# Retention and two feed-forward layers on one core: output factors kept whole in DRAM, keys loaded once, 64-row states

## The chip, the cores and the metric

The kernel runs on one core of one Trainium2 chip. The metric is the time of one execution on the device in microseconds. Before the change three executions took 1200.15, 1204.12 and 1204.95 us; the median is 1204.12 us.

## What is computed

```python
B, H, S, D = 4, 8, 768, 64            # attention part
gamma = 1.0 - 2.0 ** (-5.0 - np.arange(H))
for t in range(S):                    # retention: a decayed state per head
    state = gamma * state + outer(k[:, :, t], v[:, :, t])
    y[:, :, t] = D ** -0.5 * q[:, :, t] @ state
x = y as (B * S, H * D)               # 3072 tokens x 512
for w_in, w_out, act in ((512x2048, 2048x512, leaky_relu 0.01),
                         (512x2048, 2048x512, h * sigmoid(1.702 h))):
    x = act(x @ w_in) @ w_out
```

All results are float32. The weights of the two layers arrive as 8-byte floats and are turned into float32 on the chip.

## The kernel before, in words

**Retention.** Each sequence is cut into 6 chunks of 128 tokens, so there are 24 steps. A step loads 1 MB: queries and keys with the head dimension on the partitions (two heads stacked to 128 partitions, 4 pairs), and the keys a second time and the values with tokens on the partitions (`a_load`, L254). TensorE forms the scores of each head (L268, 64 rows each), adds `kv` from decayed keys and values (L299), the output from masked scores and values (L305), and adds queries times state (L309). The state `st` of a pair of heads is a 128x128 tile with two 64x64 blocks on its diagonal and zeros beside them; DVE writes the two blocks with two instructions (L314). Loads run four steps ahead.

**The two layers.** Every product of a layer is a two-by-two block product done in seven block products. Each float32 factor is split into a high part that the engine takes exactly (ACT copies it to the type fp32r) and a low part (DVE subtracts the high part), and three matmuls replace one. `first` (L385) is the product with `w_in` plus the activation: 4 blocks of 768 tokens, 8 pairs of column strips each, so 32 pairs; a pair is seven products of six 384-column matmuls (L410). In a pair the order on TensorE is products 1, 5, 3 (of the pair before), 6, 4 (of the pair before), 2, 7. Around them ACT copies `b<-a` (L473), DVE copies `p<-c` (L479) and adds `c<-b,p`, `g<-b,p` (L437), ACT and in layer 1 also DVE apply the activation (L416, L419, L420), and ACT's queue stores the hidden strip `g` to DRAM (`gd`, L434). `second` (L552) is the product with `w_out`: 3 blocks, seven products of eight steps of six 512-column matmuls (L601), from strips that SP loads back 13 steps ahead; DVE sums strips (L576), ACT and DVE split them (L545, L550).

**Weight preparation** (`Prep`, L96) makes the seven factors of a strip half: two loads of 256 KB, ACT and DVE turn 8-byte words to float32 (L122 to L131), POOL rounds and forms sums (L136, L141), then ACT copies the high part and DVE takes the low part (L150, L153). The result goes either straight into the resident `w` tile, or to DRAM (`store`, L156: two stores of 448 KB). All 16 halves of layer 0's `w_in` and half of layer 1's go straight to `w`; the others are stored as high and low part and loaded later, 1792 KB per strip (`loader`, L685, load at L692).

**What sets the order.** Instructions are written out by hand. `Later` is a clock of ticks: a tick is one product in `first` and one step in `second`; `later.at(n, step)` puts a step's instructions n ticks further on. `Prep.start` uses such offsets (`FAST`), and a new preparation starts every `JIT` or `STORED` ticks. `after(q)` is called when TensorE has finished product 4 of strip q in the last block; SP then loads the next product's strip q into the same `w` tile. Each engine executes its own list in order, and SP's list holds all loads and the preparation's stores.

Of the kernel before, what the change touches and what calls it, by code (L numbers as in the profile page):

```python
# [20 lines left out]
P = 128  # L21
# [33 lines left out]
class Later:  # L55


    def __init__(self):
        self.now = 0
        self.due = {}  # L60

# [3 lines left out]
    def tick(self):  # L65
        for step in self.due.pop(self.now, []):
            step()
        self.now += 1

    def drain(self):  # L70
        while self.due:
            self.tick()


@with_exitstack
def retention_two_ffn(ctx: ExitStack, tc: tile.TileContext, qkv, consts, small, w1i, w1o, w2i, w2o, scratch, out):
# [5 lines left out]
    wd = {(kind, lay): dram.tile([P, n, 2, 2, 7, P], F32, name=f"wd{kind}{lay}")  # L82
          for kind, lay, n in (("o", 0, NQ), ("i", 1, NQ // 2), ("o", 1, NQ))}
# [8 lines left out]
    later = Later()  # L92
# [3 lines left out]
    class Prep:  # L96
# [63 lines left out]

        def start(self, pool, at, dest=None):
# [4 lines left out]
            later.at(at[2], self.sums)  # L166
            later.at(at[3], lambda: self.high_part(dest))
# [6 lines left out]
    FAST = (6, 7, 8, 12, 13, 15)  # L174
# [58 lines left out]
    F_BUFS = 2  # L233
    with ExitStack() as actx:
        prep_p = prep_pool(actx)
        a_in = actx.enter_context(tc.tile_pool(name="a_in", bufs=4))
# [11 lines left out]
        st = [a_c.tile([P, NP, P], F32, name=f"st{i}") for i in range(2)]  # L248
# [5 lines left out]
        def a_load(s):  # L254
            ins[s] = a_in.tile([P, 4, 512], F32, tag="in", name="in")
            n = 2 if s < 3 else 4
            for i in range(0, 4, n):
                nc.sync.dma_start(out=ins[s][:, i : i + n], in_=qkv[s, :, i : i + n])

        def a_scores(s):  # L260
            t = ins[s]
            qT = t[:, 0].rearrange("p (n i) -> p n i", n=NP)
            kT = t[:, 1].rearrange("p (n i) -> p n i", n=NP)
            ps = [ps_a.tile([P, NP, P], F32, tag=f"s{e}", name=f"s{e}") for e in range(2)]
            for n in range(NP):
                for e in range(2):
                    r = slice(D * e, D * e + D)
                    nc.tensor.matmul(out=ps[e][:, n], lhsT=kT[r, n], rhs=qT[r, n], start=True, stop=True,  # L268
# [6 lines left out]
        def a_decay(s):  # L275
# [5 lines left out]
            if c < NC - 1:  # L281
                ks_t[s] = a_t.tile([P, H, D], F32, tag="ks", name="ks")
                nc.gpsimd.tensor_tensor(
                    out=ks_t[s], in0=ins[s][:, 2].rearrange("p (h d) -> p h d", h=H),
                    in1=kdec[:, c, :].unsqueeze(2).to_broadcast([P, H, D]), op=ALU.mult)

        def a_out(s):
# [3 lines left out]
            v = t[:, 3].rearrange("p (n f) -> p n f", n=NP)  # L291
            if c < NC - 1:
                if c == 0:
                    kv_t[b] = ps_a.tile([P, NP, D], F32, tag="kv", name="kv", bufs=2)
# [7 lines left out]
            for n in range(NP):  # L302
                for e in range(2):
                    r = slice(D * e, D * e + D)
                    nc.tensor.matmul(out=o[r, n], lhsT=v[:, n, r], rhs=sm[:, e, n], start=(n == 0),  # L305
                                     stop=(c == 0), skip_group_check=True)
            if c > 0:
                for n in range(NP):
                    nc.tensor.matmul(out=o[:, n], lhsT=st[c % 2][:, n], rhs=qs[:, n], start=False, stop=True,  # L309
                                     skip_group_check=True)  # L310
            if c < NC - 1:
                for e in range(2):
                    r = slice(D * e, D * e + D)
                    nc.vector.tensor_tensor(  # L314
                        out=st[(c + 1) % 2][r, :, r], in0=kv[r],
                        in1=gdec[r, c + 1, :].unsqueeze(2).to_broadcast([D, NP, D]), op=ALU.mult)
# [13 lines left out]
        ins[0] = a_in.tile([P, 4, 512], F32, tag="in", name="in")  # L330
        nc.sync.dma_start(out=ins[0][:, :2], in_=qkv[0, :, :2])
        nc.sync.dma_start(out=cst[:, :H], in_=consts[:, :H])
        nc.sync.dma_start(out=ins[0][:, 2:], in_=qkv[0, :, 2:])
# [3 lines left out]
        a_load(2)  # L337
        a_load(3)
# [10 lines left out]
        for i in range(2):  # L349
            nc.gpsimd.memset(st[i], 0.0)  # L350
# [3 lines left out]
        for s in range(len(steps)):  # L354
# [13 lines left out]
            if s + 4 < len(steps):  # L368
                a_load(s + 4)
# [15 lines left out]
    def first(lay, wt, blocks, g_p, prep, line, after, prepared):  # L385
# [3 lines left out]
        with ExitStack() as c:  # L389
# [24 lines left out]
            def act(src, dst):  # L414
# [393 lines left out]
```

## Time and profile before

| | |
|---|---|
| profiled execution | 1204.84 us |
| its span, first to last instruction | 1203.1 us |
| mean granted clock of TensorE | 0.96 of 2.4 GHz |
| busy PE / DVE / ACT / POOL | 1083.9 / 859.9 / 579.5 / 350.5 us |
| moved by DMA | 263.09 MB, 219 GB/s over the span |
| first product of layer 0 / second | 119.0 to 399.2 / 399.2 to 652.7 us |
| first product of layer 1 / second | 655.5 to 953.4 / 953.4 to 1203.1 us |

The retention fills the time up to 119.0 us. The mean busy shares cover stages with different limits, so they are read stage by stage. A matmul is pipelined: its listed duration overlaps the next one's, and its true rate is the distance between starts.

### The profile page before, as it was taken

The numbers are of one execution on the slowest core, as the hardware profiler recorded it, in microseconds if no ns is written. First come the engines' busy times: TensorE is split into PE (matmuls) and PEld (weight loads), VectorE is DVE, ScalarE is ACT, GpSimd is POOL, SyncE is SP. The second block draws the span as 40 slices with busy tenths as digits, with TensorE's granted clock in tenths as the row PEclk, the third lists the DMA queues.
The fourth block names the chain that finished last, engine by engine and source line by source line (L and its number), as shares of the span: only waits on it lengthen the run. The fifth ranks groups of instructions, "written<-read, shape, count | busy, mean of one in ns | idle before, by whom it ended". The sixth has DMA issues, their size and how long they took to land. (4 is left out here: it accounts for less than half of the span.)

```text
span 1203.1 us, 17472 instructions
## 1 busy us (share of the span) xinstructions
PE 1083.9 (90%) x6081; PEld 964.0 (80%) x6082; DVE 859.9 (71%) x1290; ACT 579.5 (48%) x967; POOL 350.5 (29%) x386
## 2 busy tenths in 40 slices
PE   8877989889889699999997787989989799999997
PEld 6766978879789577887885787989989688888886
DVE  5898577586763278687785599888884388687684
ACT  1333556666653244544543464565552255545543
POOL 2566475575742000000002275363540000000000
PEclk9988999999999889999999799999999899999999
DMA  8985757979889942625246653878779953624422
GB/s 312 335 310 193 243 166 233 332 252 342 306 275 370 362 162 89 227 70 179 102 140 245 210 184 131 302 241 273 255 255 349 328 171 99 214 71 137 143 71 70
DMA packets 136185, 263.09 MB, mean 219 GB/s; under 512 B 12064, under 2 KB 88352, under 8 KB 130848
## 3 DMA queue, kind: packets, MB, share of 16 engines
q1 hardware_dynamic: 99232, 211.62, 51.2%
q10 hardware_dynamic: 36864, 50.35, 11.6%
q8 instruction: 48, 0.79, 0.3%
q14 instruction: 41, 0.34, 0.1%
HBM read 157.59 MB, written 104.33 MB: 218 GB/s over the span
## 5 line engine op out<-in xcount | busy, mean ns | idle before, releaser
L545 ACT CAST op<-g 128x512 fp32r<-128x512 f32 x336 | 201.9, 622 | 189.4 <-PE f L601 50.4
L410 PE MATMUL b<-xf,w 128*128 128x384 f32 x1152 | 239.3, 353 | 54.2 <-DVE c L437 25.9
L550 DVE TENSOR_TENSOR op<-g,op 128x512 fp32r<-128x512 f32 x336 | 224.0, 689 | 61.3 <-ACT op L545 59.0
L410 PEld LDWEIGHTS b<-xf,w 128*128 128x128 f32 x1152 | 210.6, 195 | 67.6 <-DVE c L437 33.4
L410 PE MATMUL a<-xf,w 128*128 128x384 f32 x768 | 166.0, 352 | 14.8 <-DVE xf L224 10.5
L136 POOL TENSOR_TENSOR f<-f,rnd 128x512 int32<-128x512 int32 x64 | 93.0, 1453 | 241.4 <-DVE f L131 80.0
L410 PEld LDWEIGHTS a<-xf,w 128*128 128x128 f32 x768 | 144.1, 197 | 18.3 <-DVE xf L224 11.4
L576 DVE TENSOR_TENSOR g<-g 128x512 f32<-128x512 f32 x192 | 146.0, 760 | 17.3 <-DMA g<-gd 17.3
L141 POOL TENSOR_TENSOR f<-f 128x128 f32<-128x128 f32 x256 | 150.9, 610 | 10.0
L632 POOL TENSOR_TENSOR u<-u 128x1024 f32<-128x1024 f32 x6 | 16.0, 2671 | 467.3 <-DVE u L632 392.5
L601 PE MATMUL d<-op,w 128*128 128x512 f32 x576 | 140.1, 402 | 12.7 <-DVE op L550 11.6
L410 PE MATMUL c<-xf,w 128*128 128x384 f32 x768 | 150.1, 344 | 0.7 <-DVE xf L224 0.7
L601 PEld LDWEIGHTS d<-op,w 128*128 128x128 f32 x576 | 111.2, 194 | 38.6 <-DVE op L550 14.0
L601 PE MATMUL e<-op,w 128*128 128x512 f32 x576 | 136.3, 393 | 5.6 <-DVE op L550 5.6
L410 PEld LDWEIGHTS c<-xf,w 128*128 128x128 f32 x768 | 139.4, 192 | 2.1 <-DVE xf L224 2.1
L601 PE MATMUL f<-op,w 128*128 128x512 f32 x576 | 132.5, 389 | 0.0
L601 PEld LDWEIGHTS e<-op,w 128*128 128x128 f32 x576 | 108.2, 189 | 29.7 <-DVE op L550 7.3
L601 PEld LDWEIGHTS f<-op,w 128*128 128x128 f32 x576 | 108.1, 188 | 22.5
L153 DVE TENSOR_TENSOR f<-f,hi 128x896 fp32r<-128x896 f32 x40 | 53.8, 1345 | 29.2 <-ACT hi L150 29.0
L437 DVE TENSOR_TENSOR g<-b,p 128x384 f32<-128x384 f32 x64 | 35.3, 552 | 52.9 <-DMA gd<-g 29.0
L601 PE MATMUL h<-op,w 128*128 128x512 f32 x288 | 67.0, 390 | 0.0
L601 PEld LDWEIGHTS h<-op,w 128*128 128x128 f32 x288 | 53.8, 188 | 11.0
(72 smaller groups left out, 1177.1 us busy)
## 6 DMA issues: line engine op xcount, KB each, us to landing
gd<-g ACTq DMA_DIRECT2D x256, 192.0 KB, 3.9
g<-gd SPq DMA_DIRECT2D x192, 256.0 KB, 4.4
w<-wdo SPq DMA_DIRECT2D x16, 1792.0 KB, 9.5
in<-qkv SPq DMA_DIRECT2D x21, 1024.0 KB, 6.5
wdo<-hi SPq DMA_DIRECT2D x32, 448.0 KB, 3.3
wdo<-f SPq DMA_DIRECT2D x32, 448.0 KB, 3.3
xr<-xd SPq DMA_DIRECT2D x7, 1536.0 KB, 8.4
raw<-w1i SPq DMA_DIRECT2D x32, 256.0 KB, 5.7
```

What stands on the lines that cost most here:

```text
L136: nc.gpsimd.tensor_tensor(out=self.f.bitcast(I32), in0=self.f.bitcast(I32), in1=r, op=ALU.add)
L141: nc.gpsimd.tensor_tensor(out=f[:, o], in0=f[:, a], in1=f[:, b], op=ALU.subtract)
L153: nc.vector.tensor_tensor(out=self.lo, in0=self.t.bitcast(F32)[:, 1:], in1=self.hi.bitcast(F32), op=ALU.subtract)
L410: nc.tensor.matmul(out=t, lhsT=w[:, k, a], rhs=x[:, b, k], start=(start and m == 0), stop=(m == 5), skip_group_check=True)
L437: nc.vector.tensor_tensor(out=o, in0=x, in1=y, op=ALU.add)
L545: nc.scalar.copy(out=t[:, 0], in_=block_of(raw, *item))
L550: nc.vector.tensor_tensor(out=t[:, 1], in0=block_of(raw, *item), in1=t[:, 0].bitcast(F32), op=ALU.subtract)
L576: nc.vector.tensor_tensor(out=a(*s[0]), in0=a(*s[1]), in1=a(*s[2]), op=s[3])
L601: nc.tensor.matmul(out=t[:, j], lhsT=w[:, j, a], rhs=x[:, b], start=(new and q == 0 and m == 0), stop=(q == NQ - 1 and m == 2), skip_group ...
L632: put = lambda o, x, y, op=ALU.add, e=nc.vector: e.tensor_tensor(out=o, in0=x, in1=y, op=op)
```

## The change

- **Output factors whole.** For `w_out` of both layers the preparation stops after POOL's sums and stores the seven factors once as float32 (448 KB per half). `load_second` loads 896 KB per strip into the low half of `w`, and `split` makes high and low part there: ACT copies each half 5 and 6 ticks after the load's issue, DVE subtracts a tick later. These ticks run on a second clock, `loads`, which goes on from `first` into `second`. The second half of layer 1's `w_in` is still stored as two parts.
- **Keys once.** From step 2 on a step loads 768 KB; TensorE turns the keys with an identity (`a_turn`) and ACT copies them to SBUF. Steps 0 and 1 still load both forms. Loads run six steps ahead.
- **States stacked.** `st` is 128x64 per pair of heads; one DVE instruction writes it, and the product with the queries becomes 8 matmuls on 64 rows and 64 columns instead of 4 on 128x128.
- **Smaller edits.** In layer 1 the strip `g` is taken when DVE writes the gated value, not when the sigmoid is issued; layer 0 issues its store right behind the activation. Buffers and intervals change as in the diff.

```diff
@@ class Later
+        for other in self.along:
+            other.tick()
     def drain(self):
+        along, self.along = self.along, ()
...
@@ class Prep
-                self.hi = self.pool.tile([P, 7, P], F32R, tag="hi", name="hi", bufs=2)
+                self.hi = self.pool.tile([P, 8, P], U32, tag="f", name="hi", bufs=F_BUFS).bitcast(F32R)[:, 1:]
...
+        def store_whole(self):
+            nc.sync.dma_start(out=wd["o", self.lay][:, self.q, self.hh], in_=self.t.bitcast(F32)[:, 1:])
...
             later.at(at[2], self.sums)
+            if self.kind == "o":
+                later.at(at[4], self.store_whole)
+                return
...
-    FAST = (6, 7, 8, 12, 13, 15)
+    FAST = (6, 7, 8, 12, 14, 16)
@@ retention
+    LEAD = 6
-        a_in = actx.enter_context(tc.tile_pool(name="a_in", bufs=4))
+        a_in = actx.enter_context(tc.tile_pool(name="a_in", bufs=LEAD))
-        st = [a_c.tile([P, NP, P], F32, name=f"st{i}") for i in range(2)]
+        st = [a_c.tile([P, NP, D], F32, name=f"st{i}") for i in range(2)]
+        def a_turn(s):
+            t = ps_a.tile([P, NP, P], F32, tag="kt", name="kt", bufs=1)
+            for n in range(NP):
+                nc.tensor.matmul(out=t[:, n], lhsT=ins[s][:, 1, n * P : n * P + P], rhs=ident, is_transpose=True,
+                                 start=(n == 0), stop=True, skip_group_check=True)
+            kT[s] = a_t.tile([P, NP, P], F32, tag="kT", name="kT")
+            nc.scalar.copy(out=kT[s], in_=t)
...
+            if s + 2 < len(steps):
+                a_turn(s + 2)
             if c > 0:
                 for n in range(NP):
-                    nc.tensor.matmul(out=o[:, n], lhsT=st[c % 2][:, n], rhs=qs[:, n], start=False, stop=True,
-                                     skip_group_check=True)
+                    for e in range(2):
+                        r = slice(D * e, D * e + D)
+                        nc.tensor.matmul(out=o[r, n], lhsT=st[c % 2][r, n], rhs=qs[r, n], start=False, stop=True,
+                                         skip_group_check=True)
...
@@ first, layer 1's gate
+                    def product():
+                        dst = tile() if t is None else t
+                        nc.vector.tensor_tensor(out=dst, in0=src, in1=s, op=ALU.mult)
+                        later.at(2, lambda: store(dst))
+                    later.at(1, product)
@@ loads of w_out
+    def load_second(lay):
+        tiles = []
+        def after(q):
+            t = w_tile(q)
+            nc.sync.dma_start(out=t[:, :, 1].bitcast(F32), in_=wd["o", lay][:, q])
+            tiles.append(t)
+            def split(h):
+                hi, lo = t[:, h, 0], t[:, h, 1]
+                nc.scalar.copy(out=hi, in_=lo.bitcast(F32))
+                loads.at(1, lambda: nc.vector.tensor_tensor(out=lo, in0=lo.bitcast(F32), in1=hi.bitcast(F32),
+                                                            op=ALU.subtract))
+            for h in range(2):
+                loads.at(5 + h, lambda h=h: split(h))
...
-    JIT, STORED = 4.25, (5.4, 7.5)
+    JIT, STORED = 4, (4.6, 6.5, 7.5)
...
-    F_BUFS = 3
-    g_p = right.enter_context(tc.tile_pool(name="g", bufs=5, side="right", reuse_waits="tile"))
+    F_BUFS = 4
+    g_p = right.enter_context(tc.tile_pool(name="g", bufs=7, side="right", reuse_waits="tile"))
...
-    F_BUFS = 2
+    F_BUFS = 3
```

The last of these lines and a `g` pool that stays at 5 are layer 1's.

On TensorE, in a step of the retention, the list before read as follows (`st_104` is one of the two state tiles, `s_250` and `s_251` the scores of the even and odd heads):

```order
L299 MATMUL kv<-in,ks 64x64 x8
L305 MATMUL o<-sm,in 64x128 x8
L309 MATMUL o<-qs,st_104 128x128 x4
L268 MATMUL s_250<-in 128x128
L268 MATMUL s_251<-in 128x128
```

In the changed kernel the same place reads (`kt` is the PSUM tile of the turned keys):

```order
L335 MATMUL kv<-in,ks 64x64 x8
L341 MATMUL o<-sm,in 64x128 x8
L292 MATMUL kt<-a_ident,in 128x128 x4
L349 MATMUL o<-qs,st_104 64x128 x8
L304 MATMUL s_282<-in,kT 128x128
L304 MATMUL s_283<-in,kT 128x128
```

Four transposes stand between the output and the product with the state, and that product has twice as many matmuls.

On ACT, one pair in the last block of layer 0's first product read before (stores of `g` are the DMA rows):

```order
L473 COPY b<-a 128x384
L416 ACTIVATE g<-g 128x384
L434 DMA gd_62<-g 128x384
L416 ACTIVATE g<-c 128x384
L434 DMA gd_62<-g 128x384
L416 ACTIVATE g<-b 128x384
L434 DMA gd_62<-g 128x384
L416 ACTIVATE g<-a 128x384
L434 DMA gd_62<-g 128x384
```

and reads now:

```order
L514 COPY b<-a 128x384
L454 ACTIVATE g<-g 128x384
L451 DMA gd_62<-g 128x384
L454 ACTIVATE g<-c 128x384
L451 DMA gd_62<-g 128x384
L748 CAST w<-w 128x896 x2
L454 ACTIVATE g<-b 128x384
L451 DMA gd_62<-g 128x384
L454 ACTIVATE g<-a 128x384
L451 DMA gd_62<-g 128x384
```

Two copies of the split stand behind the activation of `c`; the first of them waits for the load of the strip.

On DVE, where layer 0's second product opens, the list before alternated between sums of strips and low parts:

```order
L550 TENSOR_TENSOR op<-g,op 128x512
L576 TENSOR_TENSOR g<-g 128x512
L550 TENSOR_TENSOR op<-g,op 128x512
L576 TENSOR_TENSOR g<-g 128x512
L550 TENSOR_TENSOR op<-g,op 128x512
```

and now it holds the subtractions of the last two strips of `w` as well:

```order
L617 TENSOR_TENSOR g<-g 128x512
L749 TENSOR_TENSOR w<-w 128x896
L591 TENSOR_TENSOR op<-g,op 128x512
L617 TENSOR_TENSOR g<-g 128x512
L591 TENSOR_TENSOR op<-g,op 128x512
L617 TENSOR_TENSOR g<-g 128x512
L591 TENSOR_TENSOR op<-g,op 128x512
L617 TENSOR_TENSOR g<-g 128x512
L749 TENSOR_TENSOR w<-w 128x896
L591 TENSOR_TENSOR op<-g,op 128x512
L617 TENSOR_TENSOR g<-g 128x512
L749 TENSOR_TENSOR w<-w 128x896
```

The first of the three `w` rows is strip 6's, the other two are strip 7's. Strip 7's second half now stands behind five sums of loaded strips, and the step of the product that uses it is the eighth.

## Rows read from the trace of the kernel before

**Rows 1.** Windows by stage: length; busy PE, PEld, DVE, ACT, POOL; PEclk; DMA share; GB/s

```profile
0.00:119.00 119.00, 94.66 (x1271) 79.78 (x1273) 97.23 (x149) 36.62 (x55) 63.76 (x70) 0.93 0.81 291
119.00:332.00 213.00, 190.03 (x1021) 181.85 (x1020) 149.96 (x202) 128.88 (x223) 129.95 (x149) 0.98 0.78 265
332.00:399.20 67.20, 62.17 (x330) 60.96 (x330) 30.19 (x47) 31.19 (x58) 18.49 (x24) 0.95 0.93 335
399.20:427.00 27.80, 17.53 (x51) 12.93 (x50) 8.16 (x14) 6.32 (x13) 0.00 (x0) 0.72 0.88 347
652.70:877.00 224.30, 193.11 (x1017) 186.30 (x1017) 181.40 (x277) 122.77 (x211) 108.02 (x123) 0.94 0.68 235
877.00:953.40 76.40, 64.81 (x331) 62.75 (x331) 40.36 (x72) 27.18 (x54) 9.89 (x13) 0.91 0.88 316
953.40:966.50 13.10, 11.77 (x49) 9.12 (x50) 8.25 (x15) 5.58 (x10) 0.00 (x0) 1.00 0.97 333
```

**Rows 2.** Chain that ended last: start us, us, engine, tile, line, matmul instructions

```profile
886.03 2.12 PE c L410 x12
...
977.36 10.88 PE f L601 x48
...
1095.88 1.09 PE y L617 x8
```

**Rows 3.** Timeline of PE in the retention: start us, us, line, operation, tiles, count

```profile
24.25 1.16 PE L309 MATMUL o<-qs,st 128*128 128x128 f32 x8
25.34 1.16 PE L268 MATMUL s<-in 64*128 64x128 f32 x16
26.43 0.69 PE L299 MATMUL kv<-in,ks 128*64 128x64 f32 x16
26.95 1.04 PE L305 MATMUL o<-sm,in 128*64 128x128 f32 x16
27.92 1.16 PE L309 MATMUL o<-qs,st 128*128 128x128 f32 x8
```

**Rows 4.** Windows, ten microseconds of the retention, columns as in rows 1

```profile
60.00:70.00 10.00, 6.78 (x112) 5.81 (x110) 9.86 (x13) 3.96 (x6) 8.29 (x8) 1.00 0.99 356
```

**Rows 5.** Groups by line and shape: busy us, mean ns, idle before, releasers

```profile
L153 DVE TENSOR_TENSOR f<-f,hi 128x896 fp32r<-128x896 f32 x40 | 53.8, 1345 | 29.2 <-ACT hi L150 29.0
...
L150 ACT CAST hi<-f 128x896 fp32r<-128x896 f32 x40 | 37.7, 943 | 40.2 <-POOL f L141 37.8 <-issue 1.0 <-ACT g L416 0.5
...
L314 DVE TENSOR_TENSOR st<-kv,smalls 64x256 f32<-64x256 f32 x40 | 16.7, 417 | 0.4
...
L617 PE MATMUL y<-ident,u 128*128 128x128 f32 x96 | 12.7, 275 | 1.8 <-ACT u L665 1.1 <-POOL u L632 0.7
```

**Rows 6.** Waits of PE in layer 0's first product: us in total, times, longest us

```profile
PE b L410 <- ACT b L473: 9.0, 8, 3.9
PE b L410 <- DVE c L437: 8.8, 7, 2.6
```

**Rows 7.** DMA issues in 340 to 430 us: KB each, median us to landing

```profile
w<-wdo SPq DMA_DIRECT2D x8, 1792.0 KB, 9.4
...
gd<-g ACTq DMA_DIRECT2D x31, 192.0 KB, 7.4
```

**Rows 8.** DMA issues over the whole span, columns as in rows 7

```profile
gd<-g ACTq DMA_DIRECT2D x256, 192.0 KB, 3.9
...
wdo<-hi SPq DMA_DIRECT2D x32, 448.0 KB, 3.3
```

**Rows 9.** Timeline of DVE where layer 0's second product opens, idle before in brackets

```profile
419.14 0.69 DVE L576 TENSOR_TENSOR g<-g 128x512 f32<-128x512 f32 x1 [12.10 <-DMA g<-gd]
```

**Rows 10.** Waits of DVE in layer 1's last block, columns as in rows 6

```profile
DVE g L420 <- DMA gd<-g: 16.2, 7, 3.3
DVE g L437 <- DMA gd<-g: 11.8, 3, 7.5
```

**Rows 11.** Timeline of DVE while POOL is idle

```profile
901.50 1.08 DVE L153 TENSOR_TENSOR f<-f,hi 128x896 fp32r<-128x896 f32 x1
```

More of the change, by code (lines that the diff above doesn't have):

```diff
@@ L90, in w_tile @@
         return w_p[n % NQ // (NQ // 2)].tile([P, 2, 2, 7, P], F32R, tag="w", name="w")
-    later = Later()
+    loads = Later()
+    later = Later((loads,))
     class Prep:
@@ L336, in retention_two_ffn @@
         nc.sync.dma_start(out=cst[:, H:], in_=consts[:, H:])
-        a_load(2)
-        a_load(3)
+        for s in range(2, LEAD):
+            a_load(s)
         idle = a_c.tile([P, 512], BF16, name="idle")
@@ L348, in retention_two_ffn @@
         keep_warm(8)
-        for i in range(2):
-            nc.gpsimd.memset(st[i], 0.0)
         a_scores(0)
@@ L412, in product, with hidden, relu, gate @@
                         m += 1
-            def act(src, dst):
-                if lay == 0:
+            def hidden(n, r, f, src=None, made=None):
+                blk, q = pairs[n]
+                cols = slice((2 * blk + r) * T1, (2 * blk + r + 1) * T1)
+                tile = lambda: g_p.tile([P, T1], F32, tag="g", name="g")
+                store = lambda t: nc.scalar.dma_start(out=gd[lay][f * NQ + q][:, cols], in_=t)
+                def relu(src, dst):
                     nc.scalar.activation(out=dst, in_=src, func=AF.Lrelu)
-                else:
+                    store(dst)
+                def gate(src, t):
                     s = u_p.tile([P, T1], F32, tag="sg", name="sg", bufs=3)
                     nc.scalar.activation(out=s, in_=src, func=AF.Sigmoid, scale=1.702)
-                    later.at(1, lambda: nc.vector.tensor_tensor(out=dst, in0=src, in1=s, op=ALU.mult))
-            def hidden(n, r, f, src):
-                blk, q = pairs[n]
-                t = g_p.tile([P, T1], F32, tag="g", name="g")
-                ticks = 0 if lay == 0 else 3
-                if callable(src):
-                    src(t)
-                    later.at(1, lambda: act(t, t))
-                    ticks += 1
-                else:
-                    act(src, t)
-                cols = slice((2 * blk + r) * T1, (2 * blk + r + 1) * T1)
-                later.at(ticks, lambda: nc.scalar.dma_start(out=gd[lay][f * NQ + q][:, cols], in_=t))
+                    def product():
[3 more added lines that the diff above has]
+                    later.at(1, product)
+                if made is not None:
+                    t = tile()
+                    made(t)
+                    later.at(1, lambda: relu(t, t) if lay == 0 else gate(t, t))
+                elif lay == 0:
+                    relu(src, tile())
+                else:
+                    gate(src, None)
             def add(o, x, y):
@@ L504, in first @@
                     product(cur["b"], n, 7, False)
-                    hidden(n, 1, 1, lambda t: add(t, cur["b"], cur["p"]))
+                    hidden(n, 1, 1, made=lambda t: add(t, cur["b"], cur["p"]))
                     form(7)
@@ L711, in prepared @@
         early.append(Early(left, lay))
-    tiles, after = loader("o", 0, NQ)
+    tiles, after = load_second(0)
     first(0, w1, blocks, g_p, prep_p, line, after, lambda: prepared(0))
     right.close()
-    tiles1, after = loader("i", 1, NQ // 2)
+    tiles1, after = load_first(NQ // 2)
     right = ExitStack()
@@ L736, in retention_two_ffn @@
         later.tick()
-    line = [(p, tiles1[p.q], JIT) for p in preps("i", 1)[NQ:]] + [(p, None, STORED[1]) for p in preps("o", 1)]
-    tiles, after = loader("o", 1, NQ)
+    line = [(p, tiles1[p.q], JIT) for p in preps("i", 1)[NQ:]] + [(p, None, STORED[2]) for p in preps("o", 1)]
+    tiles, after = load_second(1)
     first(1, tiles1, blocks, g_p, prep_p, line, after, lambda: prepared(1))
```

65 lines of the change are left out of this document (37 added, 28 removed).

## The prediction

> **What bounds the kernel now.** I read the windows by stage first, then the chain, then the waits of the stages that lose time. TensorE is the engine to count against. In dense stretches 12 of the 384-column matmuls take 2.12 us and 48 of the 512-column ones 10.88 us [rows 2], so a product of `first` costs 1.06 us, a pair of seven 7.42 us, a layer's 32 pairs 237.4 us, and a layer's 1008 wide matmuls 228.5 us. Set against this, the stages lose:
> - Layer 0's `first`: 213.0 us for 24 pairs (178.1), 34.9 lost, and 67.2 us for its last block (59.4), 7.8 lost [rows 1].
> - The opening of layer 0's `second`: 27.8 us for 10.88 us of matmuls, 16.9 lost at a mean granted clock of 0.72 [rows 1].
> - Layer 1's `first`, with the change of layers ahead of it: 224.3 us for 24 pairs, 46.2 lost, and 76.4 us for the last block, 17.0 lost. Its `second` opens in 13.1 us, 2.2 lost [rows 1].
>
> What is late differs by stage. Inside `first` TensorE waits for ACT's copy `b<-a` (9.0 us) and for DVE's sum `c` (8.8 us) [rows 6]: both engines work in order and stand in the weight preparation; ACT's high-part copies alone wait 37.8 us for POOL's sums [rows 5]. In both last blocks DMA is the limit: share 0.93 and 0.88 [rows 1], a load of `w` takes 9.4 us, and a 192 KB store of `g` 7.4 us there [rows 7] against 3.9 over the span [rows 8]. The stores hold the `g` buffers, and DVE in layer 1's last block waits 16.2 + 11.8 = 28.0 us for them [rows 10]. In layer 0's opening DVE waits 12.10 us for one loaded strip [rows 9], which SP issues behind the last `w` loads. The retention is two things: up to about 40 us TensorE runs without idle, 3.67 us a step (24.25 to 27.92) [rows 3]; later DVE is the bound, 9.86 us busy of 10 [rows 4].
>
> **The change part by part.** The profiled execution took 1204.84 us, of which 1203.1 is span; the sum is made against 1204.84. The median of the runs is 0.7 us lower.
>
> *Retention, -3 us.* TensorE gains 22 times four transposes. Eight of the same form take 1.09 us [rows 2], so 0.545 us a step and 12.0 us in all. The state product goes from 8 instructions in 1.09 us to 16 smaller ones; the nearest row is the output product, 16 instructions in 0.97 us (26.95 to 27.92) [rows 3], so -0.1 us a step. If twice the instructions took twice the time it would be +1.09 us on 20 steps, +21.8 us; I take the -0.1, since the output product's half-width tiles are the nearest shape. In the seven steps or so where TensorE is the bound this is +0.44 each, +3 us. DVE loses 20 of its 40 state instructions of 0.417 us [rows 5], 8.3 us; of the 16 steps where DVE is the bound that is 6.7 us, of which I keep 6, since the transposes now stand between two products that the next scores wait behind. ACT's 22 copies are hidden: it is busy 36.62 of 119 us [rows 1]. The 5.8 MB less of loads, and loads six steps ahead, I cost at nothing, as neither of the two bounds is DMA; if DMA were the bound they would be worth 5.8 MB at 291 GB/s [rows 1], 20 us. Ends: -20 and +34.
>
> The transposes have two prices in the profile: 275 ns is the mean duration of one [rows 5], 136 ns their distance [rows 2]; I use the distance, as for all matmuls. The Trainium skill (TensorE: Matmul & The Clock Gate, Part 4: PE-mode transpose) gives about 275 ns in a kernel; by that, an estimate, the 88 transposes would cost 24.2 us instead of 12.0. It also says that the clock gate doesn't count them as activity; no row here shows that, since the present ones lie between dense matmuls.
>
> *Preparation inside layer 0's `first`, -8 us.* 16 of its 32 halves lose ACT's copy (0.943 us, and 37.8/40 = 0.95 us of waiting on POOL with it) and DVE's subtraction (1.345 us) [rows 5]: 30 us of ACT's queue, 21.5 of DVE's. What TensorE can get back is what it waits for these two, 17.8 us [rows 6], with some clock. Half of the preparations change, hence about half. Ends 0 and -18. New intervals (4 and 4.6 ticks against 4.25 and 5.4) pack the remaining DVE work closer; a shorter preparation pays for it. Its changed SP list is shorter (one store for two), and the later store and the other buffer of the high part only delay data that is read a block later: nothing.
>
> *Layer 0's last block, -3 us.* Eight `w` loads shrink from 1792 to 896 KB, 7.3 MB of the 22.5 MB that the 335 GB/s over 67.2 us make [rows 1]; the `g` stores get faster and the pool has seven buffers for five. Ends 0 and -7.8. The block takes on 16 copies (15.1 us) and 16 subtractions, 1.08 us each while POOL is idle [rows 11], 17.3 us; ACT and DVE are busy 31.19 and 30.19 of 67.2 [rows 1], so they fit. The new wait is ACT's, for the load. The split comes five ticks after the issue, 5.3 us. A 448 KB store lands in 3.3 us [rows 8], a 1792 KB load in 9.4 [rows 7]; I take 5. Behind it wait the activations, and TensorE waits for `b<-a`, five products on (5.3 us, less 1.9 of copies): a landing of up to 8.3 us still hides.
>
> *Layer 0's opening, -12 us.* The strip that DVE waits for stands behind 3.7 instead of 7.3 MB of the last four `w` loads, 10.6 us at 347 GB/s [rows 1] instead of 21. What is late next is the split itself: strip 7's second half is ready for TensorE's eighth step (9.5 us in) only after five sums and three subtractions of DVE, each sum behind a load. I leave 5 of the 16.9 us. Ends 0 and -16.9.
>
> *Layer 1's `first`, -3 and -10 us.* The first 24 pairs lose the same 21.5 us of DVE, in a stage where it is busy 181.4 of 224.3 us [rows 1]; but most of the loss lies at the layer change and where `w` is still prepared just in time, which are untouched: -3, ends 0 and -15. In the last block the stores' 28.0 us of DVE waits go for the most part. But DVE, busy 40.36 us [rows 1], takes on 17.3 us of subtractions, less the two preparations' 2.2: 55.5 of the ideal 59.4. I leave 7 of the 17.0 lost. Ends 0 and -17. The later taking of `g` buffers is part of this.
>
> *Layer 1's opening, +3 us.* The list is layer 0's, so 5 us lost instead of 2.2.
>
> Sum: -3 -8 -3 -12 -3 -10 +3 = -36, 1204.84 - 36 = 1168.8, by the median 1168.
>
> **The rivals.**
> *The last blocks stay late, now for DVE.* For it: 55.5 of 59.4 us leaves little room, and at the mean 1.345 us a subtraction [rows 5] it is 59.8, over the bound. Against: POOL is busy only 9.89 of 76.4 us there [rows 1]. Both last blocks and layer 0's opening then give half, 12.5 us less: 1181.
> *The retention gets longer.* TensorE is busy 94.66 of 119 us [rows 1]; with +12.0 us it comes near the bound on every step, and the gain on DVE goes into waiting for turned keys. Against: the DVE bound in [rows 4]. +12 instead of -3 gives 1183, with the state product at twice its time up to 1205. The Trainium skill's price of a transpose, above, points this way.
> *The change doesn't buy what its bytes promise.* SP issues the strips only after TensorE's last product whatever the loads weigh; then the opening and the blocks keep their time and 25 us fall away: 1193. Against: the `g` stores at 7.4 instead of 3.9 us, which depend on load.
> *More than half goes.* If TensorE is held up by nothing but these waits, and the half clock goes with them, the ends of layer 0 (-18, -7.8, -16.9) and layer 1 (-17, -3) give about -60: 1145.
> *Slower: ACT stands at the split.* With a landing L after issue ACT is blocked L - 5.3 us a pair and has 4.4 us of its own (four activations of about 0.5, a copy of 0.5, two of 0.943 [rows 5]); above L = 8.3 us the pair is longer than 7.42, 16 times. At L = 11 that is +43 us, the gains at the blocks and openings (-22) are gone, and the rest (-14) stays: 1234. It makes the kernel slower than before from L = 9.2. For it: 9.4 us for the present load [rows 7]. Against: that is twice the bytes.
>
> **How the numbers follow.** Forecast 42 %, its own range 1156 to 1182. DVE in the last blocks 14 %, retention 12 %, bytes off the path 10 %, more than half 15 %, ACT at the split 7 %. The range that leaves out 2 in 10 is 1143 to 1197. A measurement of this kernel can tell about 0.5 % from no change, 6 us. Faster: all of the forecast, of the larger gain and of the DVE case, 11 of the retention's 12 and 5 of the bytes' 10: 0.87. No change: the others of these two, 0.06. Slower: 0.07.
>
> **What would show it.** Right: DMA share in the last blocks falls below 0.8 and `g` stores land in under 5 us; DVE's waits for `gd<-g` fall below 10 us; the opening of layer 0's `second` takes under 17 us; TensorE's waits for `b<-a` and `c` in layer 0's `first` halve; the retention ends between 111 and 120 us. Wrong: ACT idle in front of the split for several microseconds a pair, the retention beyond 125 us, or openings as long as before.

## The result, and the profile after

The changed kernel takes 1187.31 us (median of four runs, 1183.3 to 1189.15) beside 1203.93 for the one before on the same chip: a ratio of 0.9863, interval 0.9829 to 0.9897. That is 16.6 us less where 36 were forecast: the direction held, the size did not. The time lies outside the forecast's own range (1156 to 1182) and inside the wide one (1143 to 1197). The profiled execution took 1189.15 us, 1187.4 of it span, against 1204.84 and 1203.1. Stage times below are those of one execution each. Executions of the changed kernel lie up to 5.9 us apart, and the profiled one is the longest of the four, so a microsecond or two in a stage counts only where other runs repeat it.

The table cuts each stage at the same matmul in both kernels: the first of a product, and the one at three quarters of `first` (24 of 32 pairs). These cuts lie up to some five microseconds from the round ones of [rows 1].

| stage | before, us | after, us | predicted | measured |
|---|---|---|---|---|
| retention | 119.0 | 122.7 | -3 | +3.7 |
| layer 0 `first`, 24 pairs | 208.3 | 211.4 | -8 | +3.1 |
| layer 0 `first`, last block | 71.9 | 71.1 | -3 | -0.8 |
| layer 0 `second`, up to layer 1's first matmul | 256.3 | 248.5 | -12 | -7.8 |
| layer 1 `first`, 24 pairs | 220.1 | 211.5 | -3 | -8.6 |
| layer 1 `first`, last block | 77.8 | 65.5 | -10 | -12.3 |
| layer 1 `second` and the end | 249.7 | 256.6 | +3 | +6.9 |

The forecasts of -12 and +3 were made for the openings of `second` alone. The openings went from 27.5 us (at the new cut) to 19.0 and from 13.1 to 16.9: -8.5 and +3.8. The rest of the two rows, +0.7 and +3.1, lies behind the openings.

The windows of the changed kernel by these stages, columns as in [rows 1]; the second line is the retention from step 2 on, the third answers to [rows 4], and the sixth and the last are the two openings of `second`:

```profile
0.00:122.70 122.70, 104.02 (x1520) 83.39 (x1520) 88.32 (x130) 48.29 (x77) 63.78 (x70) 0.99 0.72 235
20.20:122.70 102.50, 89.94 (x1429) 75.68 (x1428) 83.28 (x123) 45.93 (x74) 59.95 (x61) 1.00 0.68 218
60.00:70.00 10.00, 8.91 (x144) 7.46 (x142) 8.33 (x14) 5.24 (x9) 6.79 (x10) 1.00 0.84 264
122.70:334.10 211.40, 191.68 (x1013) 186.15 (x1012) 131.16 (x188) 117.66 (x209) 126.30 (x156) 0.95 0.72 239
334.10:405.20 71.10, 63.12 (x337) 61.85 (x337) 41.02 (x56) 39.70 (x68) 13.52 (x16) 0.95 0.78 266
405.20:424.20 19.00, 14.18 (x50) 9.55 (x49) 12.79 (x19) 9.97 (x16) 0.00 (x0) 0.82 0.83 275
...
653.80:865.30 211.50, 190.92 (x1011) 185.46 (x1012) 159.11 (x262) 106.85 (x194) 107.72 (x123) 0.95 0.64 215
865.30:930.80 65.50, 60.44 (x338) 59.09 (x337) 50.20 (x81) 35.28 (x63) 11.51 (x13) 1.00 0.75 248
930.80:947.70 16.90, 11.99 (x49) 8.99 (x49) 14.31 (x22) 9.57 (x15) 0.00 (x0) 0.96 0.89 292
```

The same view of the kernel before, from step 2 of the retention on and for layer 0's 24 pairs at the new cut:

```profile
14.30:119.00 104.70, 84.01 (x1185) 74.19 (x1185) 92.15 (x141) 34.75 (x53) 60.45 (x62) 0.92 0.80 286
119.00:327.30 208.30, 188.60 (x1014) 180.72 (x1013) 145.34 (x196) 125.43 (x217) 127.61 (x146) 0.98 0.78 265
```

*Retention.* From step 2 on it gains 2.2 us (104.7 to 102.5), close to the forecast of 3; TensorE, not DVE, is now the fullest engine of a steady stretch (8.91 of 10 us). The time is lost before step 2. TensorE's timeline of the changed kernel at the start, columns as in [rows 3]:

```profile
14.69 1.12 PE L292 MATMUL kt<-a_ident,in 128*128 128x128 f32 x4 [2.76 <-DMA in<-qkv]
17.45 1.45 PE L304 MATMUL s<-in,kT 64*128 64x128 f32 x16
...
20.22 1.16 PE L304 MATMUL s<-in,kT 64*128 64x128 f32 x16
...
22.80 0.66 PE L292 MATMUL kt<-a_ident,in 128*128 128x128 f32 x4
23.39 1.09 PE L349 MATMUL o<-qs,st 64*64 64x128 f32 x16
```

And of the kernel before:

```profile
11.83 1.16 PE L268 MATMUL s<-in 64*128 64x128 f32 x16
...
14.33 1.16 PE L268 MATMUL s<-in 64*128 64x128 f32 x16
```

The turning of step 2 (the transposes of L292 at 14.69) stands ahead of the scores of step 1 and waits for step 2's load. The scores of step 1 (11.83 before, 17.45 now) need neither; those of step 2 start 5.9 us later, and 5.9 - 2.2 is the 3.7 of the table. The last two rows show a later step: its four transposes take the 0.59 us between the two starts.

*Layer 0's `first`.* The four largest waits of TensorE in the 24 pairs, before, which split those of [rows 6]:

```profile
PE b L410 <- DVE c L437: 8.8, 7, 2.6
PE b L410 <- DVE xf L224: 4.4, 2, 3.1
PE b L410 <- ACT b L473: 4.0, 5, 2.1
PE a L410 <- ACT w L150: 1.6, 2, 1.3
```

After:

```profile
PE b L442 <- DVE c L478: 7.7, 8, 2.0
PE b L442 <- ACT b L514: 5.5, 5, 2.3
PE a L442 <- DVE w L160: 3.4, 1, 3.4
PE b L442 <- ACT xf L236: 2.5, 1, 2.5
```

DVE lost 14.2 us of work here and ACT 7.8, of 21.5 and 15.1 that the change takes out; the closer intervals also bring preparation into these pairs that fell in the last block before, where POOL works 13.52 us instead of 20.83. The four waits sum to 19.1 us instead of 18.8, and the mean granted clock is 0.95 instead of 0.98. Over the whole `first` the two rows of [rows 6] sum to 17.4 us, 17.8 before. In the other runs with the new intervals and offsets (e1 to e3, e8 to e11) these pairs take 208.7 to 211.2 us, so no gain shows in any of them, and the loss is between nothing and 3 us. In the last block there is a new stop. SP's timeline, then ACT's and TensorE's (three views of the changed kernel; on SP the span covers issues that wait for each other):

```profile
374.41 8.83 SPq L577 DMA_DIRECT2D g<-gd  x8
383.47 4.91 SPq L743 DMA_DIRECT2D w<-wdo  x2
```

```profile
392.51 1.78 ACT L748 CAST w<-w 128x896 fp32r<-128x896 f32 x2 [5.68 <-DMA w<-wdo]
```

```profile
397.54 3.64 PE L442 MATMUL b<-xf,w 128*128 128x384 f32 x12 [4.26 <-ACT b L514]
```

Eight loads of strips stand on SP ahead of a load of `w`; the split on ACT stands 5.68 us, and TensorE loses 4.26 us for the copy `b<-a` behind it.

*Openings.* DVE's timeline where layer 0's second product opens, which answers to [rows 9]:

```profile
414.02 0.69 DVE L617 TENSOR_TENSOR g<-g 128x512 f32<-128x512 f32 x1 [2.66 <-DMA g<-gd]
...
419.69 0.69 DVE L617 TENSOR_TENSOR g<-g 128x512 f32<-128x512 f32 x1
420.30 1.09 DVE L749 TENSOR_TENSOR w<-w 128x896 fp32r<-128x896 f32 x1
421.30 0.69 DVE L591 TENSOR_TENSOR op<-g,op 128x512 fp32r<-128x512 f32 x1
```

The wait of 12.10 us is gone, and 2.66 us is the longest that DVE still stands for a strip; L749, the split's subtraction, now stands between the sums. TensorE's largest waits in the two openings, layer 0's and then layer 1's:

```profile
PE d L642 <- DVE op L591: 2.4, 2, 2.1
PE d L642 <- DVE w L749: 2.1, 2, 1.5
...
PE d L642 <- DVE w L749: 3.4, 2, 2.2
```

L591 is the subtraction that splits a sum of strips. The loss doesn't end with the opening. TensorE's next product in layer 1, 48 matmuls that took 10.88 us from start to start before and take 13.55 now (947.73 to 961.28):

```profile
947.73 13.71 PE L642 MATMUL e<-op,w 128*128 128x512 f32 x48
```

The mean granted clock in it is 0.79, against 1.00 in the kernel before, with TensorE busy throughout in both. These 2.7 us are most of the 3.1 behind layer 1's opening. They are not in every run: in e10 and e3 the product takes 10.9 us, behind openings of 16.5 and 17.4.

*Layer 1's last block* is where the change pays most. DVE's waits there had two rows on stores of `g`, 28.0 us [rows 10]; now the largest row is:

```profile
DVE w L749 <- ACT w L748: 4.7, 2, 3.9
```

The loads and stores that answer to [rows 7], in 345 to 435 us and in 877 to 945:

```profile
w<-wdo SPq DMA_DIRECT2D x8, 896.0 KB, 7.1
gd<-g ACTq DMA_DIRECT2D x32, 192.0 KB, 5.2
...
w<-wdo SPq DMA_DIRECT2D x8, 896.0 KB, 5.7
gd<-g ACTq DMA_DIRECT2D x32, 192.0 KB, 4.5
```

The load lands in 7.1 us at the median, more than the 5 I took and less than the 8.3 that would still hide. Of the groups that answer to [rows 5], the transposes:

```profile
L292 PE MATMUL kt<-a_ident,in 128*128 128x128 f32 x88 | 14.9, 293 | 2.8 <-DMA in<-qkv 2.8
```

### The profile page after: what moved, and what is told of

It is laid out like the page before. It is cut to its first block, busy times and chain, and to the rows that moved or that the text cites. A ratio compares the mean times of both kernels' runs of the same rounds, so it can differ in the third digit from the quotient of the medians.

```text
span 1187.4 us, 17984 instructions
## 1 busy us (share of the span) xinstructions
PE 1091.3 (92%) x6330; PEld 968.7 (82%) x6330; DVE 840.7 (71%) x1270; ACT 590.4 (50%) x989; POOL 343.2 (29%) x386
## 4 chain that ended last, share of the span: by engine, by line
PE 54%; DVE 9%; DMA 6%; ACT 4%; issue 3%; POOL 3%; ACTq 1%; POOLq 0%; SPq 0%; DVEq 0%
PE f L642 11%; PE d L642 9%; PE e L642 9%; PE b L442 9%; PE h L642 6%; PE a L442 5%; PE c L442 4%; DMA gd<-g 2%; DMA w<-wdo 1%; DMA xd<-u 1%; DVE xf L237 1%; POOL f L148 1%; DVE f L134 1%; ACT g L454 1%; DVE g L617 1%
## 5 line engine op out<-in xcount | busy, mean ns | idle before, releaser
L586 ACT CAST op<-g 128x512 fp32r<-128x512 f32 x336 | 202.3, 622 | 177.2 <-PE f L642 50.4
L442 PE MATMUL b<-xf,w 128*128 128x384 f32 x1152 | 240.7, 355 | 41.2 <-ACT b L514 15.1
L591 DVE TENSOR_TENSOR op<-g,op 128x512 fp32r<-128x512 f32 x336 | 225.2, 691 | 63.4 <-ACT op L586 62.3
L442 PEld LDWEIGHTS b<-xf,w 128*128 128x128 f32 x1152 | 213.5, 198 | 53.5 <-ACT b L514 19.8
L442 PE MATMUL a<-xf,w 128*128 128x384 f32 x768 | 162.0, 347 | 14.4 <-DVE xf L237 10.1
L143 POOL TENSOR_TENSOR f<-f,rnd 128x512 int32<-128x512 int32 x64 | 87.8, 1372 | 227.3 <-DVE f L138 91.9
L642 PE MATMUL d<-op,w 128*128 128x512 f32 x576 | 137.5, 395 | 9.7 <-DVE w L749 5.5
L642 PE MATMUL e<-op,w 128*128 128x512 f32 x576 | 141.0, 403 | 4.4 <-DVE op L591 4.4
L642 PEld LDWEIGHTS d<-op,w 128*128 128x128 f32 x576 | 108.4, 189 | 35.8 <-DVE w L749 7.8
L642 PEld LDWEIGHTS e<-op,w 128*128 128x128 f32 x576 | 111.6, 195 | 29.7 <-DVE op L591 6.3
L134 DVE TENSOR_SCALAR f<-f 128x512 f32<-128x512 f32 x64 | 38.9, 608 | 46.9 <-ACT f L130 32.7
L129 ACT ACTIVATE rnd<-raw 128x512 int16<-128x512 uint32 x64 | 50.5, 789 | 26.0 <-POOL f L143 10.3
```

Of the source, the lines that this page charges most:

```text
L129: nc.scalar.activation(out=rnd[:, :, 0], in_=raw[:, :, 0], func=AF.Copy, scale=2.0**-29)
L134: nc.vector.tensor_scalar(out=f.bitcast(F32), in0=f.bitcast(F32), scalar1=HW_MIN, scalar2=HW_MAX, op0=ALU.max, op1=ALU.min)
L143: nc.gpsimd.tensor_tensor(out=self.f.bitcast(I32), in0=self.f.bitcast(I32), in1=r, op=ALU.add)
L442: nc.tensor.matmul(out=t, lhsT=w[:, k, a], rhs=x[:, b, k], start=(start and m == 0), stop=(m == 5), skip_group_check=True)
L586: nc.scalar.copy(out=t[:, 0], in_=block_of(raw, *item))
L591: nc.vector.tensor_tensor(out=t[:, 1], in0=block_of(raw, *item), in1=t[:, 0].bitcast(F32), op=ALU.subtract)
```

## The experiments

Each edit is to the changed kernel unless another is named, and ratios are to the kernel before. "Quarters" are those of a `first`, eight pairs each; in the changed kernel 71.8, 70.7, 68.9, 71.2 us in layer 0 and 81.3, 64.4, 65.8, 65.5 in layer 1.

**e1: the retention of before.** The retention's block is taken from the kernel before, all else is the changed kernel.

> The changed kernel with the retention of the kernel before (keys loaded twice, 128x128 states, loads four steps ahead); the layers are the changed ones. The changed kernel's retention ended at 122.7 us, the one of before at 119.0. Theory A (the retention's change costs time by itself): 1184 us, 3 to 4 us below the changed kernel's 1187, with the retention ending at 119. Rival B (the retention's end only shifts what the layers lose anyway, or its lighter loads help what follows): 1187 or more.

1183.76 us, 0.9837 [0.9799, 0.9875]; the retention ends at 119.5. The new retention costs some 3.5 us, and what follows takes the same within 2 us. By the medians alone the spread of the runs would hide 3.5 us; the end of the retention shows it: 121.1 to 122.8 us in the six kernels that keep the new order (e3, e4, e6, e8, e11 and the changed one), 117.8 to 118.3 in the five with the edit of e2.

**e2: the turn of step 2 behind the scores of step 1.**

```diff
-            if s + 2 < len(steps):
+            if 0 < s and s + 2 < len(steps):
                 a_turn(s + 2)
...
                 a_scores(1)
+                a_turn(2)
```

> The changed kernel with one instruction group moved: the turning of step 2's keys stands behind step 1's scores instead of ahead of them. In the changed kernel TensorE waits there 2.8 us for the load and then works at half clock; step 1's scores start at 17.5 us against 11.8 before. Theory A (the loss at the start comes from the order on TensorE): step 1's scores start before 14 us, the retention ends 3 to 5 us earlier, 1183 us. Rival B (the loads themselves are late, whatever stands ahead): the retention ends where it did, 1187.

1183.85 us, 0.9837 [0.9796, 0.9878]. The retention ends at 117.8, 1.2 us ahead of the kernel before. TensorE's timeline there:

```profile
12.10 1.16 PE L304 MATMUL s<-in,kT 64*128 64x128 f32 x16
13.36 0.66 PE L292 MATMUL kt<-a_ident,in 128*128 128x128 f32 x4
...
15.24 1.16 PE L304 MATMUL s<-in,kT 64*128 64x128 f32 x16
```

The transposes wait for nothing, and step 2's scores start at 15.24 instead of 20.22. The cost was the place in the list, not the transposes.

**e3: the eight early strip loads spread**, one per two ticks instead of all at once.

```diff
-            for item in ITEMS[:NQ]:
-                load_block(lay, self.raw, {"x": self.x}, *item)
+            for k, item in enumerate(ITEMS[:NQ]):
+                later.at(2 * k, lambda item=item: load_block(lay, self.raw, {"x": self.x}, *item))
```

> The changed kernel with the eight early loads of strips issued one every two ticks instead of all at once, in both layers. In the changed kernel they hold SP from 374.4 to 383.2 us ahead of a load of w, and ACT then waits 5.7 us for that load in front of the split, TensorE 4.3 us for ACT. Theory A (SP's order makes the load late): ACT's longest wait in front of the split falls below 2 us, and the kernel takes 1181 us (4 us of idle and 2 of clock less). Rival B (DMA's rate in that stretch is the limit, not the order): the wait stays over 4 us and the time 1187.

1178.61 us, 0.9795 [0.9766, 0.9824]. Layer 0's last block as a window:

```profile
333.10:399.40 66.30, 62.02 (x339) 60.76 (x338) 41.28 (x56) 39.98 (x69) 13.55 (x16) 0.97 0.86 291
```

The block falls from 71.1 to 66.3 us, and ACT's waits at the split in it from 7.8 to 2.1: the strip loads on SP were what it stood for.

**e4: the old intervals.** Ticks between preparations and the offsets in them as before.

```diff
-    FAST = (6, 7, 8, 12, 14, 16)
+    FAST = (6, 7, 8, 12, 13, 15)
...
-    JIT, STORED = 4, (4.6, 6.5, 7.5)
+    JIT, STORED = 4.25, (5.4, 5.4, 7.5)
```

> The changed kernel with the preparation's intervals and offsets of before (4.25 and 5.4, 5.4, 7.5 ticks; low part a tick earlier). Layer 0's first product took 282.5 us in the changed kernel and 280.2 before, though ACT and DVE have 30 and 21 us less to do in it. Theory A (the closer intervals ate the gain): that product falls to 276 us or less, the kernel to 1181. Rival B (the gain was never there, since TensorE's waits come from the preparation's other instructions): the product stays at 281 to 284, the kernel at 1187 or above.

1192.1 us, 0.9894 [0.9863, 0.9926]. Layer 0's quarters are 70.0, 68.6, 63.7, 79.8, layer 1's first is 88.2. Windows of layer 0's 24 pairs and last block:

```profile
121.10:323.40 202.30, 186.76 (x1013) 180.12 (x1012) 126.81 (x180) 112.45 (x201) 121.00 (x146) 0.98 0.72 236
323.40:403.20 79.80, 64.91 (x338) 62.71 (x337) 49.01 (x65) 44.67 (x76) 24.11 (x26) 0.91 0.79 274
```

The two largest of TensorE's waits in those 24 pairs (the next two are 2.7 and 1.0 us):

```profile
PE b L442 <- DVE c L478: 5.3, 4, 2.6
PE b L442 <- ACT b L514: 5.0, 4, 3.1
```

At the old spacing the 24 pairs gain 6.0 us on the kernel before, with TensorE's four largest waits 14.0 us instead of 18.8. But preparation moves into the last block, where POOL works 24.11 us instead of 13.52 and TensorE stops once for 8.17 us behind the split. The stage takes 282.2 us, as in the changed kernel (282.5). The rival's numbers hold, but not its reason: the gain was there, and the last block lost it.

**e5: e2 and e3 together, with the old intervals in layer 0 alone.** Layer 1 keeps 4 ticks and the new offsets.

> The changed kernel with three edits together: step 2's keys turned behind step 1's scores; early strips issued one every two ticks; the preparation's intervals and offsets of before in layer 0 only (layer 1 keeps 4 and 7.5 ticks). With the intervals of before alone, the first 24 pairs of layer 0 took 202 us (211 in the changed kernel, 208 before), and its last block 80 (71, 72), with one stop of 8.2 us in front of the split. Theory A (the factors' lighter preparation is worth some 6 us at the old intervals, and the last block's loss was SP's order): layer 0's first product 270 us, the kernel 1168 to 1172. Rival B (the old intervals only push preparation work into the last block, which has no room beside the split): the product stays at 276 or more, the kernel at 1175.

1176.18 us, 0.9769 [0.9745, 0.9794]. Quarters of 71.5, 68.5, 63.7, 72.9, 276.6 in all, against 277.0 in e3: with TensorE's longest stop behind ACT in the last block down from 8.17 to 1.9 us, wider spacing only moves time from the third quarter to the last. The rival holds.

**e6: the old offsets alone** (`FAST` of e4).

> The changed kernel with the offsets of before alone (low part 13 instead of 14 ticks behind the load, store 15 instead of 16); intervals as changed. With intervals and offsets of before the first quarter of layer 1's first product took 87.7 us, as before (87.1), against 80.7 in the changed kernel. Theory A (the interval of 4 ticks is the cause): the quarter stays at 81 and the kernel at 1186 to 1188. Rival B (the later low part is the cause): the quarter goes to 87, the kernel to 1193.

1189.67 us, 0.9883 [0.9851, 0.9915]. Layer 1's first quarter stays at 82.8 (88.2 in e4, 87.7 before): the interval of 4 ticks brings this gain, not the offsets. Layer 0's 24 pairs stay at 211.2 us, so there too the 202.3 of e4 come from the intervals.

**e7: the kernel before with that interval** (4.25 becomes 4, nothing else).

> The kernel before with one number changed: a new just-in-time preparation every 4 ticks instead of 4.25. Theory A (4 ticks by themselves shorten layer 1's first quarter, and the changed kernel's gain there is not the factors'): that quarter falls from 87 to 81 us, the kernel to 1197. Rival B (it needs the third buffer or the later low part of the changed kernel): 1203, the quarter at 87.

1218.42 us, 1.0127 [1.0096, 1.0159], slower. Layer 1's first quarter gains (84.3 against 87.7), but layer 0's quarters are 72.4, 74.3, 76.1, 69.1, and the second and the last of layer 1 lose as well. Its window of layer 0's 24 pairs, to be set beside 208.3 us at 0.98:

```profile
120.20:343.00 222.80, 194.39 (x1014) 188.86 (x1013) 145.40 (x202) 127.43 (x220) 127.01 (x151) 0.93 0.74 253
```

The same work, 14.5 us longer, with TensorE's waits for `c` 17.3 us instead of 8.8. Neither theory had that. Only eight preparations of each layer's `first` come every 4 ticks; in layer 0 the 24 behind them keep their 5.4 and merely start two ticks earlier. So how the preparation falls against the pairs of seven ticks matters by several microseconds a quarter; by what mechanism is not shown.

**e8: no low part for the last two strips.** Eight of DVE's 32 split subtractions are left out, four a layer; in these strips the whole factor stands where the low part should.

```diff
-                loads.at(1, lambda: nc.vector.tensor_tensor(out=lo, ...
+                if q < NQ - 2:
+                    loads.at(1, lambda: nc.vector.tensor_tensor(out=lo, ...
```

> The changed kernel without DVE's subtractions for strips 6 and 7 of the output factors, in both layers; their low part is left as the whole factor, so part of the computation is wrong. In the changed kernel the opening of the second product took 19.0 us in layer 0 and 16.9 in layer 1 for 10.9 us of matmuls, before 27.5 and 13.1. Theory A (the split's subtractions on DVE, between sums that wait for strips, hold TensorE): both openings lose 3 to 4 us, the kernel 1181 or, with the half clock that follows, 1179. Rival B (the strips' loads set it): openings of 18 and 16 us, the kernel 1186.

1173.14 us, 0.9742 [0.9715, 0.977]. The openings take 13.7 and 12.3 us instead of 19.0 and 16.9; layer 0's `second` up to layer 1 takes 241.5 us instead of 248.5, layer 1's 249.3 instead of 256.6. TensorE's timeline in layer 0's opening:

```profile
402.48 2.92 PE L642 MATMUL d<-op,w 128*128 128x512 f32 x12
406.03 7.17 PE L642 MATMUL d<-op,w 128*128 128x512 f32 x30 [0.63 <-DVE op L591]
```

Four subtractions of 1.1 us cost 7 us a layer where the stages meet, about twice what theory A had: 5.3 and 4.6 us in the openings, and the rest behind them, where the next product runs at the full clock here (10.9 us in both layers).

**e9: e2 and e3, and POOL subtracts for the last two strips.**

```diff
-                loads.at(1, lambda: nc.vector.tensor_tensor(out=lo, ...
+                e = nc.gpsimd if q >= NQ - 2 else nc.vector
+                loads.at(1, lambda: e.tensor_tensor(out=lo, ...
```

> The changed kernel with step 2's keys turned behind step 1's scores, the early strips issued one every two ticks, and the low parts of strips 6 and 7 of the output factors taken by POOL instead of DVE. POOL is idle where the second products open; a subtraction of 128x768 takes it 2.0 to 2.3 us, so 128x896 some 2.5 us. Leaving these subtractions out brought the openings from 19.0 and 16.9 us to 13.7 and 12.3 and the kernel 14 us. Theory A (what holds TensorE there is DVE's list, not the load): openings of 15 and 14 us, the kernel 1168. Rival B (POOL is late itself, or slows DVE's sums beside it): openings of 18 and 17 us, 1176.

1178.76 us, 0.9796 [0.9772, 0.982]; openings of 18.7 and 17.4. One of POOL's subtractions in layer 0's opening runs from 410.69 for 2.10 us; DVE's timeline at the same time:

```profile
410.77 2.57 DVE L618 TENSOR_TENSOR g<-g 128x512 f32<-128x512 f32 x1
```

POOL takes twice as long as DVE, and the sum that runs beside it 2.57 us instead of 0.69. The rival holds; e10, the same kernel without this edit, is no slower.

**e10: e2 and e3 together.**

> The changed kernel with the first two of these edits only: keys turned behind the scores, early strips spread. Alone they gave 3.5 and 8.7 us. Theory A (they lie at different places and add up): 1175 to 1177, the retention ending at 118, layer 0's last block 66 us. Rival B (an earlier end of the retention is lost again in layer 0's first product): 1178 to 1180.

1176.31 us, 0.9783 [0.9762, 0.9803]; the retention ends at 118.2, layer 0's last block takes 66.4. The two edits add up. This and e5, within 0.2 us of each other, beat both kernels.

**e11: each strip of `w_out` loaded twice**, 1792 KB again.

```diff
-            nc.sync.dma_start(out=t[:, :, 1].bitcast(F32), in_=wd["o", lay][:, q])
+            for half in range(2):
+                nc.sync.dma_start(out=t[:, :, half].bitcast(F32), in_=wd["o", lay][:, q])
```

> The changed kernel with each load of an output-factor strip done twice, once into the high half (which ACT overwrites) and once into the low half: 1792 KB as before, with everything else as changed. Theory A (the bytes are what the last blocks and the first opening gained from): layer 1's last block goes from 65.5 us to 72 or more (78 before), stores of g take over 6 us there, the kernel 1198 or more. Rival B (the gain came from the stores and preparation left out, or from the buffers; the loads' bytes don't matter): block below 68 us, the kernel below 1192.

1209.74 us, 1.0056 [1.0038, 1.0074]. Last blocks of 83.0 and 73.6 us (71.1 and 65.5 with one load), openings of 20.1 and 19.6. ACT's wait around layer 0's last block:

```profile
ACT w L749 <- DMA w<-wdo: 15.0, 3, 8.5
```

DVE's waits for stores of `g` in layer 1's last block:

```profile
DVE g L463 <- DMA gd<-g: 2.4, 2, 1.3
```

Loading them twice costs 22 us on the changed kernel, but the way was not the one expected: stores of `g` land in 4.8 us in layer 1's last block, and it is ACT that stands at the split, which needs both loads. DVE's 28.0 us of waits for these stores [rows 10] don't come back with the bytes. So the lighter loads alone don't explain why they went; the later taking of `g` and the preparation that fell away came with the same change, and no run here parts them.

**e12: e10 with the last two strips of each layer stored and loaded as two parts**, as before.

> The kernel with both order edits (keys turned behind the scores, early strips spread, 1176 us) in which strips 6 and 7 of the output factors are stored and loaded as high and low part, as before the change, and strips 0 to 5 whole. The openings then have no split to wait for, at the price of 1.8 MB more in loads per layer and eight more high and low parts in the preparation. Theory A (the split's place in the openings costs more than its bytes): openings near 14 us, as without those subtractions, the kernel 1166. Rival B (the two full loads in the last block make the strips behind them as late): openings of 18 us or more, the kernel 1176 or above.

1181.34 us, 0.9823 [0.9793, 0.9852]; openings of 18.4 and 16.6. DVE's timeline in layer 0's:

```profile
410.81 0.69 DVE L619 TENSOR_TENSOR g<-g 128x512 f32<-128x512 f32 x1 [6.16 <-DMA g<-gd]
```

Without the four subtractions DVE waits for strips again, behind two full loads. The rival holds: the opening is bound either way.

## Why the forecast was right or wrong

**The retention, -3, became +3.7.** The step's terms held nearly: four transposes take 0.59 us of a step (22.80 to 23.39 in the changed kernel, 0.545 forecast), DVE is off the bound, and from step 2 on 2.2 us are gained. "Loads six steps ahead I cost at nothing" failed at the start, where none is ahead yet: step 2's turn stands in TensorE's list before step 1's scores. e2 takes that back.

**Layer 0's 24 pairs, -8, became +3.1: the main failure.** "Half of the preparations change, hence about half" of the waits. In the third quarter, with the old spacing, some of that comes (63.7 us in e4, 68.4 before). But the intervals, which I cost at nothing ("a shorter preparation pays for it"), moved the work together again, and the waits were as long as before (19.1 us, 18.8 before). e4 and e5 show that the other choice gives the time to the last block: with nothing else in the way, layer 0's `first` takes 277.0 us (e3) or 276.6 (e5) against 280.2 before. So of the 11 us forecast for the stage these two settings give 3 to 4. Why these waits follow the phase of the preparation (e6, e7) is open.

**Layer 0's last block, -3, became -0.8.** DMA eased as forecast (share 0.78, stores of `g` 5.2 us instead of 7.4). e11 loses 11.9 us in this block, but by ACT's waits at the split, so it doesn't show that the bytes held the block before. My working of ACT's new wait used a landing time from issue and not what SP issues first. The rival "ACT stands at the split" cost TensorE one stop here, not 16; e3 takes it out.

**The opening, -12, became -7.8, and layer 1's, +3, became +6.9.** The mechanism, splits between sums that wait for loads, was the right one; "I leave 5" was too little in layer 0. The opening measured 19.0 us, 8.1 over 10.88, and layer 1's 6.0 over, which is nearly the forecast 5. What the forecast lacked in layer 1 is the 3.1 us behind the opening, 2.7 of them at a lower clock in the next product; that part comes and goes between runs, as e3 and e10 don't show it. e8 prices the subtractions at 7.0 and 7.3 us. Moving the work to POOL (e9) or loading parts instead (e12) gives nothing.

**Layer 1's `first`, -13, became -20.9.** The last block held nearly in size: 12.3 against 10. DVE's waits for stores went, as forecast, but e11 leaves open whether the bytes took them away. The clock is 1.00 there, DVE is busy 50.20 of 65.5 us and not the bound, which falsifies the first rival. The 24 pairs gained 8.6 instead of 3, 6.4 of it in the first quarter, which I called untouched: it was touched by the interval of 4 (e4 and e6; in the kernel before, e7, it gives 3.4).

Of the five signs named, three failed: the opening under 17 us (19.0), halved waits in layer 0 (17.4 of 17.8 us left), the retention in 111 to 120 (122.7). DVE's waits for `gd<-g` fell below 10 us as said, and so did the DMA share below 0.8; the stores under 5 us held in layer 1 (4.5), not quite in layer 0 (5.2).

On the price of a transpose: the retention lasted longer, as the Trainium skill's figure of about 275 ns (TensorE: Matmul & The Clock Gate, Part 4: PE-mode transpose) would have it, but for another reason. That figure is near the mean duration of one here (293 ns); what a transpose cost in the list is the distance, 0.15 us. The same part of the Trainium skill also says that transposes don't count as activity for the clock; with 88 of them the retention's mean granted clock was 0.99 here, 0.93 before [rows 1], so no loss shows in this kernel.

Open, and not tried: strips loaded ahead of the last loads of `w`; a spacing tuned to the phase of the pairs; the later taking of `g` without the lighter loads.

## What to carry to other kernels

An instruction that waits on a load costs what stands behind it in its engine's list, so follow each new wait through every in-order list, the one that issues the load included: two such places cost 11 us (e10), where 20 were missing, and both went by reordering. Work taken out of a stage gives time only where waits fall; price the spacing that is edited with it, or hold it still. Work moved from a spread-out stage to a transition can cost more than its own length: here four subtractions of 1.1 us cost 7. And where several things change at once, put them back one at a time before one is called the cause: the bytes came back in e11, the waits they were blamed for did not.

## What the hardware showed that I had not expected

- DVE's sum of two 128x512 tiles took 1.75 and 2.57 us beside a POOL subtraction of 128x896, and 0.69 alone (e9); the subtraction took 1.1 us on DVE and 2.1 on POOL. Both sums end 0.55 us after the subtraction beside them (413.34 after 412.79, 409.04 after 408.49), as if they had waited for its end.
- A quarter of a tick in one interval, in the kernel before, costs 1.3 % (e7).
- Behind an opening with short stops TensorE's next product, 48 matmuls without a gap, took 13.55 us at a mean granted clock of 0.79 in layer 1, and 10.88 at 1.00 in the kernel before.
